# Attention scores in one plain float32 product per head, two heads side by side on the rows of TensorE, and attention under the same list schedule as the layers behind it

## The chip, the core and the metric

The kernel runs on one NeuronCore of a Trainium2 chip. A core has TensorE (PE in the profile, with PEld for its weight loads), VectorE (DVE), ScalarE (ACT), GpSimd (POOL) and SyncE (SP), which issues DMAs here. PSUM has eight banks of 128 partitions by 512 float32. The metric is the device time of one execution in microseconds, lower is better.

## What is computed

Attention with rotary embedding on 2 x 8 heads, 576 positions, 64 features a head; its output, as 1152 tokens by 512 features, goes through two feed-forward layers.

```python
q_rot, k_rot = (rotate(q), rotate(k))
scores = scale * np.matmul(q_rot, k_rot.transpose(0, 1, 3, 2))
scores = scores - np.max(scores, axis=-1, keepdims=True)
attn = np.exp(scores)
attn = attn / (np.sum(attn, axis=-1, keepdims=True) + 1e-09)
return np.matmul(attn, v).astype(np.float32)
...
h = np.maximum(x @ w_in, 0.0)
return (h * h @ w_out).astype(np.float32)
...
a = x @ w_a
b = x @ w_b
return (a * b @ w_out).astype(np.float32)
```

Queries, keys, values and the output are float32; the weights are float64, come as int64 bit patterns and are turned into float32 parts on the chip.

## The kernel before

**Attention** works on eight pairs of heads. The two heads of a pair lie on partitions 0 to 63 and 64 to 127. For each pair the rotated queries and keys are made from `X` (loaded by `load_qk`) by a multiplication with cosines and sines and an addition. From the second pair on this is `prepare` (L305 on): the keys' half on POOL, the queries' half on DVE (L307, L308). Then ACT rounds them to fp32r (`hi`, L309), POOL takes the rest (`lo`, L310), and four DMAs (`place`) put the parts into the tile `sk`, so that the 128 rows of TensorE hold both parts of one head. The first pair does the same by hand in `first_pair` (L316 on), without DMAs.

A pair has nine score blocks (`emit_S`, L365): eight of 128 queries of one head by 576 keys, four matmuls of 288 columns each (two parts of the keys times two banks), and a ninth with the last 64 queries of both heads, ten matmuls. A block goes through a row maximum on DVE (L374) and an exponential on ACT (L380, tile `P`), is transposed on TensorE three blocks later (`emit_T`, `LT = 3`: L435, the odds and ends L445 and L449), copied out of PSUM by ACT or DVE (`evac`), and multiplied with the values (`av_units`: L477 for each head on 64 columns of the array, both heads into the two halves of one bank; L472 for the last 64 keys), first for 384 queries, then for 192. The products of `emit_scale` (L402, L410) spread the reciprocal of the row sums. The transposes and the spreads share two PSUM banks, `av` has two more and the scores four (two blocks).

Only the first three blocks' instructions stand in written order (`in_order`). Behind them the framework's scheduler orders all attention instructions.

**The feed-forward layers** (L660 to L662, L869 to L871) are ordered by `Plan`, a list scheduler in the kernel with costs, due times and buffers (`Plan.order`); what it decides is issued under a manual schedule. It starts where attention ends. Every product is made of three fp32r products. Weights pass through `convert` (three instructions on DVE, two on ACT) and `two_parts`; four of them are made during attention.

Of the kernel before, what the change touches and what calls it, by code (L numbers as in the profile page):

```python
# [16 lines left out]
P = 128  # L17
S = 576
# [9 lines left out]
LT = 3  # L28
DM = 512
NWA = 4  # L30
NWB = 8
NG = 5
NV = 3
LEAD = 40.0
HB = 288

# [11 lines left out]
class Op:  # L48
    def __init__(self, engines, cost, fn, deps, acq, rel, k):
        self.engines, self.cost, self.fn, self.k = engines, cost, fn, k  # L50
        self.deps, self.acq, self.rel = list(deps), list(acq), list(rel)
        self.end = None
# [5 lines left out]
class Plan:  # L58


    HOP = 0.1

    def __init__(self, room):
        self.ops = []
        self.free = {t: [0.0] * n for t, n in room.items()}

    def late(self, *tags, at):
        self.start = at
        for t in tags:
            self.free[t] = [at] * len(self.free[t])  # L70
# [7 lines left out]
    def takes(e, cost):  # L78
        if cost is None:
            return 0.0  # L80
        kind, n = cost[0], cost[1] / 1000
        if kind == "mm":
            return cost[2] * (n / 2.4 + 0.0134)
# [8 lines left out]
    def order(self):  # L92
# [13 lines left out]
        def due(o):  # L106
            stack = [o]
            while stack:
# [10 lines left out]
                late = min((y.due - self.HOP - (2.0 if e == "SP" else 0) for y in nexts[id(x)]), default=clock + 5) - self.takes(e, x.cost)  # L119
                x.due = min(late, x.due) if "PE" in x.engines else late  # L120

# [38 lines left out]
        while True:  # L160
# [5 lines left out]
            for e in engines[1:]:  # L166
                first = None
                for o in open_[e]:
                    if o.end is not None:
                        continue  # L170
                    r = room(o)
                    if r is None:
                        continue
                    s = max(at[e], ready[id(o)], r)
                    if first is None or (s, o.due) < first[:2]:
                        first = (s, o.due, o, e)
# [13 lines left out]
            hop = 0.0 if e == "-" else 2.0 if e == "SP" else self.HOP  # L190
# [25 lines left out]
def attention_moe_moe2_kernel(ctx: ExitStack, tc: tile.TileContext, qk, rope, vm, vt, ident_in, sel_in, w_in, w_out, w_a, w_b, w2_out, out):  # L216
# [3 lines left out]
    xpool = ctx.enter_context(tc.tile_pool(name="xpool", bufs=1))  # L220
    raw = ctx.enter_context(tc.tile_pool(name="raw", bufs=3))
    g2 = ctx.enter_context(tc.tile_pool(name="g2", bufs=2))
    ga = ctx.enter_context(tc.tile_pool(name="ga", bufs=1))
    tmp = ctx.enter_context(tc.tile_pool(name="tmp", bufs=1))
    wa = ctx.enter_context(tc.tile_pool(name="wa", bufs=NWA))

    X = {1: xpool.tile([P, 2, 2, S], F32, tag="x", name="X1")}
    xall = xpool.tile([P, NTB, 2, KC, TB], F32R, tag="x", name="x")
    xb = [xall[:, n] for n in range(NTB)]

    def psum_s(name):
        return ps.tile([P, 2, 512], F32, tag="s", name=name)

    def psum_1(tag, name):
        return ps.tile([P, 512], F32, tag=tag, name=name)
# [761 lines left out]
```

## Time and profile before

| what | us |
| --- | --- |
| median of 3 runs (602.7 to 603.99) | 603.72 |
| the profiled execution | 603.05 |
| its span, first to last instruction | 601.3 |
| PE busy (share of the span) | 574.1 (95%) |
| DVE busy | 450.8 (75%) |
| ACT busy | 341.6 (57%) |
| POOL busy | 257.3 (43%) |

Times of the trace are counted from the first instruction of the span. A row of the timeline gives the start, the time to the modelled end, the engine, the line, the operation and what it writes and reads; an instruction that begins before the one ahead has ended overlaps it, so how long a group holds TensorE is read from its start to the next group's start. A plain float32 matmul leaves two records (two matmuls of one instruction of the kernel), an fp32r matmul one.

### The profile page before, as it was taken

To read this page: it belongs to the slowest core of one execution; us is meant where nothing else is said; L and a number is where in the kernel's file an instruction comes from. 1 tells how busy PE (TensorE), PEld (TensorE's weight loads), DVE (VectorE), ACT (ScalarE), POOL (GpSimd) and SP (SyncE) were. 2 spreads that over 40 slices of the span, in tenths; PEclk is the share of its full clock that TensorE was granted. 3 is DMA by queue.
4 is the path that set the end of the run, shared out by engine and by line. 5 is a ranking of instruction groups with operands and counts; after the bars stand their busy time and mean duration, and the time that the engine had idled before them with its cause. 6 is when DMAs were issued, how large, how long until landed. Compare 5 with 4: busy or idle time off the path is not lost.

```text
span 601.3 us, 9575 instructions
## 1 busy us (share of the span) xinstructions
PE 574.1 (95%) x3554; PEld 505.9 (84%) x3554; DVE 450.8 (75%) x743; ACT 341.6 (57%) x738; POOL 257.3 (43%) x275
## 2 busy tenths in 40 slices
PE   2689999999999999999999999999999999999997
PEld 1557566666758999999999999989999999999986
DVE  5967777767535986884696387999888989897554
ACT  4649667788755876870482155457774555554110
POOL 2755556731122652450252045577554655652100
PEclk9989999999999999999999999999999999999999
DMA  7467575746001354441242031023333232320004
GB/s 244 143 177 198 149 197 127 205 135 179 21 2 67 108 166 153 138 141 35 71 141 71 1 106 36 1 70 99 113 106 105 72 106 71 105 71 2 1 0 158
DMA packets 20682, 61.46 MB, mean 102 GB/s; under 512 B 3337, under 2 KB 3721, under 8 KB 19739
## 3 DMA queue, kind: packets, MB, share of 16 engines
q1 hardware_dynamic: 20491, 59.67, 32.7%
q10 hardware_dynamic: 144, 1.18, 0.6%
q8 instruction: 28, 0.46, 0.3%
q14 instruction: 19, 0.16, 0.1%
HBM read 48.16 MB, written 2.36 MB: 84 GB/s over the span
## 4 chain that ended last, share of the span: by engine, by line
PE 85%; DVE 10%; ACT 2%; issue 1%; DMA 1%; SPq 0%; ACTq 0%; DVEq 0%
PE av L477 7%; PE s L365 7%; PE h L660 6%; PE h L661 6%; PE h L662 6%; PE y L660 5%; PE y L661 5%; PE y L662 5%; PE t L435 4%; PE o L871 4%; PE o L870 4%; PE o L869 4%; PE al L660 4%; PE al L661 4%; PE al L662 4%; DVE X L307 2%
## 5 line engine op out<-in xcount | busy, mean ns | idle before, releaser
L568 POOL TENSOR_TENSOR g<-v,g 128x384 fp32r<-128x384 f32 (+1 forms) x47 | 56.8, 1212 | 60.3 <-ACT g L571 60.2
L365 PE MATMUL s<-sk 128*128 128x288 f32 x336 | 65.7, 325 | 16.4 <-ACT sk L341 10.3
L365 PEld LDWEIGHTS s<-sk 128*128 128x128 f32 x336 | 49.0, 196 | 35.5 <-ACT sk L341 11.2
L374 DVE TENSOR_REDUCE st<-s 128x1 f32<-128x576 f32 x72 | 53.9, 753 | 32.9 <-PE s L365 32.5
L660 PE MATMUL y<-g,w_o 128*128 128x384 f32 (+1 forms) x208 | 66.9, 322 | 0.0
L662 PE MATMUL y<-g,w_o 128*128 128x384 f32 (+1 forms) x208 | 66.9, 322 | 0.0
L661 PE MATMUL y<-g,w_o 128*128 128x384 f32 (+1 forms) x208 | 66.9, 322 | 0.0
L660 PE MATMUL h<-x,w_i 128*128 128x384 f32 x192 | 64.2, 335 | 0.0
L661 PE MATMUL h<-x,w_i 128*128 128x384 f32 x192 | 64.1, 334 | 0.0
L662 PE MATMUL h<-x,w_i 128*128 128x384 f32 x192 | 64.1, 334 | 0.0
L380 ACT ACTIVATE P<-s,st 128x576 f32<-128x576 f32 x72 | 53.7, 746 | 16.7 <-DVE st L374 16.5
L660 PE MATMUL al<-y,w_p 128*128 128x288 f32 x192 | 56.9, 296 | 2.2 <-DVE v L836 2.2
L661 PE MATMUL al<-y,w_p 128*128 128x288 f32 x192 | 56.6, 295 | 0.0
L662 PE MATMUL al<-y,w_p 128*128 128x288 f32 x192 | 56.5, 294 | 0.0
L571 ACT CAST g<-v 128x384 fp32r<-128x384 f32 (+1 forms) x72 | 40.3, 564 | 24.8 <-DVE v L840 17.7
L477 PE MATMUL av<-PT,V 128*64 128x384 f32 (+1 forms) x256 | 50.7, 428 | 0.0
L435 PE MATMUL t<-ident,P 128*128 128x128 f32 x288 | 46.9, 286 | 1.2 <-ACT P L380 1.0
L418 ACT COPY PT<-t 128x512 f32<-128x512 f32 (+1 forms) x57 | 31.7, 556 | 23.3 <-PE t L435 22.6
L709 DVE TENSOR_TENSOR oacc<-o,oacc 128x512 f32<-128x512 f32 (+1 forms) x46 | 31.0, 675 | 17.6 <-PE o L871 17.2
L871 PE MATMUL o<-w,g 128*128 128x512 f32 (+1 forms) x110 | 43.1, 392 | 0.0
L870 PE MATMUL o<-w,g 128*128 128x512 f32 (+1 forms) x110 | 42.9, 390 | 0.0
L869 PE MATMUL o<-w,g 128*128 128x512 f32 (+1 forms) x110 | 42.6, 387 | 0.0
(149 smaller groups left out, 1560.9 us busy)
## 6 DMA issues: line engine op xcount, KB each, us to landing
raw_i<-in_w_in SPq DMA_DIRECT2D x16, 512.0 KB, 3.6
raw_o<-in_w_out SPq DMA_DIRECT2D x16, 512.0 KB, 3.3
X<-in_qk SPq DMA_DIRECT2D x6, 1152.0 KB, 5.2
raw_b<-in_w_b SPq DMA_DIRECT2D x12, 512.0 KB, 3.3
raw_a<-in_w_a SPq DMA_DIRECT2D x12, 512.0 KB, 3.3
raw<-in_w_out SPq DMA_DIRECT2D x12, 512.0 KB, 3.2
sk<-hi_lo SPq DMA_DIRECT2D x14, 432.0 KB, 4.6
sk<-hi_lo SPq DMA_DIRECT2D x14, 288.0 KB, 6.0
```

The lines of the kernel that those rows point to most:

```text
L365: pe.matmul(s[:, b, c:c + n], lhs, rhs, start=(m < 2), stop=(m >= len(mm) - len(cuts)), skip_group_check=(j == 8))
L374: dve.tensor_reduce(out=ST[p][:, 0, j:j + 1], in_=SP[i][:, :, 0:288], op=ALU.max, axis=AX.XY, negate=True)
L380: act.activation(pr[:, h, :].rearrange("p (b n) -> p b n", b=2), SP.pop(i)[:, :, 0:288], AF.Exp, bias=st[:, 0, j:j + 1], scale=1.0, accum_ ...
L435: pe.transpose(t[:, k * P:(k + 1) * P], flat[:, c0:c0 + P], ident)
L477: pe.matmul(AVT[p, r][half(h), 0:n], V[p][:, h, k, :], PT[p][:, h, k, q0:q0 + n], start=False, stop=(k == 3), skip_group_check=True)
L568: e.tensor_tensor(out=out_, in0=a, in1=b, op=ALU.subtract)
L660: pe.matmul(dst, wh, mh, start=first, stop=False, skip_group_check=open_)
L661: pe.matmul(dst, wh, ml, start=False, stop=False, skip_group_check=open_)
L662: pe.matmul(dst, wl, mh, start=False, stop=last, skip_group_check=open_)
L869: pe.matmul(b(), gt[:, 0, c], w[:, 0, d], start=(k == 0), stop=False)
L870: pe.matmul(b(), gt[:, 0, c], w[:, 1, d], start=False, stop=False)
L871: pe.matmul(b(), gt[:, 1, c], w[:, 0, d], start=False, stop=(k == H - 1))
```

## The change

The score product takes the rotated queries and keys as they are, in plain float32: 64 rows of the array for one head, the other 64 for the other head, alternating, into two PSUM tiles (`scores`, L351 of the changed kernel; the last 64 queries of both heads in L346). The rounding, the rest, the DMAs of the parts, `first_pair` and the zero fills are gone. The unit is now a chunk of 128 queries of both heads, four to a pair, and the tail chunk of 64.

From the second pair on POOL does the whole rotation (L317, L318); for the first pair `Plan` divides it between DVE and POOL. All attention instructions become operations of `Plan`, with the costs of the diff, and the list schedule runs from the first instruction to the last. The values are multiplied in two halves of 288 queries, each in two parts (`times_v`, L428, L430), both heads always one behind the other. PSUM holds three score tiles of two banks and two banks for all else (transposes, `av`, spreads). The probabilities have seven buffers; the last pair's spreads come behind the first product of the feed-forward layers. Seven weight slots lie apart from attention's memory instead of four; as before four weights are converted during attention (`EARLY`).

```diff
 H = 2
-LT = 3
 DM = 512
-NWA = 4
-NWB = 8
+NWA = 7
+NWB = 5
+NP = 7
+NS = 3
 NG = 5
 NV = 3
-LEAD = 40.0
 HB = 288
+QS = 192
+EARLY = 4
+GATE = (3, 0)
...
+    HOP = {"PE": 0.25, "SP": 2.0, "-": 0.0}
...
+    STAGS, TTAGS = tuple(f"s{k}" for k in range(NS)), ("t0", "t1")
...
+        if p:
+            for qi in (1, 0):
+                m = pl.op("POOL", ("s", 2 * S), lambda e, qi=qi: e.tensor_tensor(out=x()[:, :, qi, :], in0=x()[:, :, qi, :], in1=cs, op=ALU.mult), [done[qi, 0]])
+                r[qi] = pl.op("POOL", ("s", S), lambda e, qi=qi: e.tensor_tensor(out=rot[:, qi, :], in0=x()[:, 0, qi, :], in1=x()[:, 1, qi, :], op=ALU.add), [m] + war)
+            r[2] = r[0]
...
+    def scores(p, c):
+        rot = ROT[p % 2]
+        if c == 0:
+            rotate(p)
...
+        tail = c == 4
+        s = [Buf(STAGS, {t: (lambda t=t, h=h: ps.tile([P, 2, 512], F32, tag=t, name=f"s{p}_{c}_{h}")) for t in STAGS}) for h in range(1 if tail else 2)]
+        SB[p, c] = s
...
+        def mm(e):
+            k0 = [rot[half(h), 1, :] for h in range(2)]
+            if tail:
+                q0 = (rot[half(0), 0, 512:576], rot[half(1), 0, 0:64])
+                for h, bk, c0, kk, n in ((0, 0, 0, 0, 288), (1, 1, 0, 352, 224), (1, 1, 224, 0, 64), (0, 1, 0, 288, 288), (1, 0, 0, 64, 288)):
+                    pe.matmul(s[0]()[half(h), bk, c0:c0 + n], q0[h], k0[h][:, kk:kk + n], start=True, stop=True, skip_group_check=True)
+            else:
+                for bk in range(2):
+                    for h in range(2):
+                        q0 = rot[half(h), 0, 64 * h + c * P:64 * h + (c + 1) * P]
+                        pe.matmul(s[h]()[:, bk, 0:288], q0, k0[h][:, bk * 288:bk * 288 + 288], start=True, stop=True)
...
+        o = pl.op("PE", ("us", 1.1), mm, [r[1], r[0]] + ([r[2]] if c else []), acq=s)
+        SDONE[p, c] = o
...
+        for h in range(len(s)):
+            j = 2 * c + h
+            m = pl.op("DVE", ("p", S), lambda e, h=h, j=j: e.tensor_reduce(out=st()[:, 0, j:j + 1], in_=s[h]()[:, :, 0:288], op=ALU.max, axis=AX.XY, negate=True), [o])
+            x = pl.op("ACT", ("us", 0.86), lambda e, h=h, j=j: e.activation(
+                PP[:, pr.k, h, :].rearrange("p (b n) -> p b n", b=2), s[h]()[:, :, 0:288], AF.Exp,
+                bias=st()[:, 0, j:j + 1], scale=1.0, accum_out=st()[:, 1, j:j + 1]), [m], acq=[pr] if h == 0 else [], rel=[s[h]])
+            ex.append(x)
...
+    def fill(p, name, blocks, after, outs):
+        b = bank_t(name)
...
-    def prepare(p, engs):
-        x = X[p]
-        for qi in (1, 0):
-            engs[qi].tensor_tensor(out=x[:, :, qi, :], in0=x[:, :, qi, :], in1=cs, op=ALU.mult)
-            engs[qi].tensor_tensor(out=rot[:, qi, :], in0=x[:, 0, qi, :], in1=x[:, 1, qi, :], op=ALU.add)
-            act.copy(hi[qi], rot[:, qi, :])
-            pool.tensor_tensor(out=lo[qi], in0=rot[:, qi, :], in1=hi[qi].bitcast(F32), op=ALU.subtract)
-        place(p)
...
-    def emit_S(i):
-        p, j = divmod(i, 9)
...
-        heads = (j % 2,) if j < 8 else (0, 1)
-        mm = []
...
-        for h in heads:
-            q0 = MAIN[h] + (j // 2) * P if j < 8 else (512, 0)[h]
-            lhs = sk[:, h, q0:q0 + P]
-            cuts = ((0, 0, 288, 0), (1, 0, 288, 288))
-            if j == 8 and h == 1:
-                cuts = ((0, 0, 288, 64), (1, 0, 224, 352), (1, 224, 64, 0))
-            for rhs in (sk[:, h, KOFF[h]:KOFF[h] + S], sk[:, h, LOFF[h]:LOFF[h] + S]):
-                mm += [(b, c, n, lhs, rhs[:, k:k + n]) for b, c, n, k in cuts]
-        for m, (b, c, n, lhs, rhs) in enumerate(mm):
-            pe.matmul(s[:, b, c:c + n], lhs, rhs, start=(m < 2), stop=(m >= len(mm) - len(cuts)), skip_group_check=(j == 8))
...
+    def times_v(p, r, part):
...
+        def mm(e, ks, last):
+            for k in ks:
+                for h in range(2):
+                    pe.matmul(b()[half(h), 0:288], v[:, h, k, :], pt[:, h, k, q], start=(k == 0), stop=False, skip_group_check=True)
+            if last:
+                pe.matmul(b()[:, 0:288], VT[p % 2], ptt[:, q], start=False, stop=True, skip_group_check=True)
...
-        def main(r, k):
-            q0, n = RANGE[r]
-            for h in range(2):
-                pe.matmul(AVT[p, r][half(h), 0:n], V[p][:, h, k, :], PT[p][:, h, k, q0:q0 + n], start=False, stop=(k == 3), skip_group_check=True)
...
+    scores(0, 0)
+    for n, (p, c) in enumerate(order):
+        if n + 1 < len(order):
+            scores(*order[n + 1])
...
+        mid = []
+        if p:
+            mid = [lambda: times_v(p - 1, c // 2, c % 2)] if c < 4 else [lambda: flip(p - 1), lambda: spread(p - 1, 0), lambda: spread(p - 1, 1)]
+        fills = [lambda k=k: turned(p, c, k) for k in range(3 if c == 3 else 2)]
+        if c == 4:
+            mid[:1] and mid.pop(0)()
+        for f in fills:
+            f()
+            if mid:
+                mid.pop(0)()
+        for f in mid:
...
+    for n, (fn, *a) in enumerate(steps):
         fn(*a)
-
...
+        if n == 0:
+            spread(p, 0)
+            spread(p, 1)
+            pl.op(None, None, None, [x for r in range(2) for x in XS[p, r]], rel=[held("g4")])
...
-    in_order = ExitStack()
-    in_order.enter_context(tc.manual_schedule(engines={getattr(mybir.EngineType, e) for e in ("PE", "Activation", "DVE", "Pool")}))
-    pl.run({"PE": pe, "ACT": act, "DVE": dve, "POOL": pool, "SP": nc.sync})
-    in_order.close()
+    with tc.manual_schedule(engines={getattr(mybir.EngineType, e) for e in ("PE", "Activation", "DVE", "Pool")}):
+        pl.run({"PE": pe, "ACT": act, "DVE": dve, "POOL": pool, "SP": nc.sync})
```

On TensorE, in the seventh and eighth pair (`s` scores, `t`, `tk` transposes, `av` the product with the values). Before, around the eighth score block of the last pair and up to its ninth:

```order
L435 MATMUL t_1728<-ident,P_1_1654 128x128 x4
L477 MATMUL av_0_1719<-PT_1467,V_1528 64x384 x4
L365 MATMUL s_1742<-sk_93 128x288 x4
L435 MATMUL t_1750<-ident,P_1_1654 128x128 x4
L445 MATMUL tk_1756<-ident,P_0_1619 128x128
L445 MATMUL tk_1756<-ident,P_1_1654 128x128
L477 MATMUL av_0_1719<-PT_1467,V_1528 64x384 x4
L365 MATMUL s_1764<-sk_93 128x288 x5
```

After, for the last pair, from its third chunk's scores to the next:

```order
L351 MATMUL s_2_0_1350<-rot 128x288
L351 MATMUL s_2_1_1352<-rot 128x288
L351 MATMUL s_2_0_1350<-rot 128x288
L351 MATMUL s_2_1_1352<-rot 128x288
L370 MATMUL t_1_0_1357<-small,P 128x128 x4
L428 MATMUL av_0_1334<-PT_wb,V 64x288 x4
L430 MATMUL av_0_1334<-small 128x288
L370 MATMUL t_1_1_1372<-small,P 128x128 x4
L351 MATMUL s_3_0_1379<-rot 128x288
```

The scores stand in fours of two heads, with a transpose group, half of an `av` and a second transpose group between them. In the third pair of the kernel before, `av` was cut in other places, also between the two heads:

```order
L477 MATMUL av_0_619<-PT_360,V_416 64x384
L402 LDWEIGHTS part_0_605
L402 MATMUL r_0_612<-ident,part_0_605 18x128
L435 MATMUL t_628<-ident,P_1_554 128x128 x4
L477 MATMUL av_0_619<-PT_360,V_416 64x384 x2
```

After, each `av` part is a row of four, as `av_0_1334` above. On DVE at the start of attention, before (`X` and `cs_rot` the rotation, `sk` the parts, `st` the row maxima):

```order
L326 TENSOR_TENSOR X_98<-X_98,cs_rot 128x576 x2
L327 TENSOR_TENSOR cs_rot<-X_98 128x576
L326 TENSOR_TENSOR X_98<-X_98,cs_rot 128x192 x2
L327 TENSOR_TENSOR cs_rot<-X_98 128x192
L342 TENSOR_TENSOR sk_92<-cs_rot,sk_92 64x576
L343 TENSOR_TENSOR sk_92<-cs_rot,sk_92 64x192
L342 TENSOR_TENSOR sk_92<-cs_rot,sk_92 64x576
L343 TENSOR_TENSOR sk_92<-cs_rot,sk_92 64x192
L374 TENSOR_REDUCE st_146<-s_136 128x1
L326 TENSOR_TENSOR X_98<-X_98,cs_rot 128x384 x2
```

After, on DVE from its first instruction, and the shares of POOL behind it:

```order
L323 TENSOR_TENSOR X_77<-X_77,cs_rot 128x576 x2
L323 TENSOR_TENSOR X_77<-X_77,cs_rot 128x192
L324 TENSOR_TENSOR cs_rot<-X_77 128x576
L323 TENSOR_TENSOR X_77<-X_77,cs_rot 128x384
L358 TENSOR_REDUCE st_100<-s_0_0_92 128x1
L358 TENSOR_REDUCE st_100<-s_0_1_94 128x1
```

```order
L323 TENSOR_TENSOR X_77<-X_77,cs_rot 128x192
L324 TENSOR_TENSOR cs_rot<-X_77 128x192
L323 TENSOR_TENSOR X_77<-X_77,cs_rot 128x384
L324 TENSOR_TENSOR cs_rot<-X_77 128x384
L317 TENSOR_TENSOR X_88<-X_88,cs_rot 128x2x576 x2
L318 TENSOR_TENSOR rot<-X_88 128x576 x2
```

The subtractions and roundings into `sk` are gone from the start; half of the first queries' rotation and all of the second pair's (`X_88`) is on POOL. Behind the first product of the feed-forward layers and the last pair's spreads, TensorE's instructions are the same in the same order.

## Rows read from the trace of the kernel before

**Rows 1.** Windows of the span: length, busy time of each engine, PEclk, DMA share, GB/s.

```profile
0.00:10.27 10.27, 0.00 (x0) 0.03 (x1) 4.27 (x8) 3.06 (x5) 3.19 (x14) 1.00 0.72 240
10.27:33.13 22.86, 15.44 (x78) 12.57 (x78) 20.99 (x29) 14.46 (x32) 11.52 (x6) 1.00 0.60 176
33.13:185.85 152.72, 148.54 (x941) 98.18 (x941) 100.17 (x179) 104.04 (x259) 69.07 (x105) 0.99 0.49 132
185.85:601.30 415.45, 410.12 (x2539) 395.14 (x2538) 325.39 (x528) 220.08 (x444) 173.50 (x150) 1.00 0.26 84
```

**Rows 2.** Waits of PE in the feed-forward layers: us in total, times, longest.

```profile
PE al L660 <- DVE v L836: 2.2, 3, 0.9
```

**Rows 3.** Timeline of PE in the seventh and eighth pair.

```profile
151.31 1.43 PE L365 MATMUL s<-sk 128*128 128x288 f32 x10
152.57 0.66 PE L435 MATMUL t<-ident,P 128*128 128x128 f32 x4
...
156.28 0.60 PE L435 MATMUL t<-ident,P 128*128 128x128 f32 x4
156.81 0.55 PE L477 MATMUL av<-PT,V 128*64 128x192 f32 x4
157.28 0.80 PE L365 MATMUL s<-sk 128*128 128x288 f32 x4
157.91 0.60 PE L435 MATMUL t<-ident,P 128*128 128x128 f32 x4
158.35 0.38 PE L445 MATMUL tk<-ident,P 128*128 128x128 f32 x2
...
163.08 0.81 PE L472 MATMUL av<-PTT,vtail 128*128 128x384 f32 x2
163.82 0.22 PE L402 MATMUL r<-ident,part 128*18 128x128 bf16 x1
...
168.44 1.51 PE L477 MATMUL av<-PT,V 128*64 128x384 f32 x8
169.88 1.42 PE L365 MATMUL s<-sk 128*128 128x288 f32 x10
```

**Rows 4.** Timeline of PE in the second and third pair.

```profile
33.13 0.78 PE L365 MATMUL s<-sk 128*128 128x288 f32 x4
...
63.46 0.22 PE L402 MATMUL r<-ident,part 128*18 128x128 bf16 x1 [1.16 <-DVE PT L420]
...
65.97 0.86 PE L477 MATMUL av<-PT,V 128*64 128x384 f32 x2
66.76 0.66 PE L435 MATMUL t<-ident,P 128*128 128x128 f32 x4
```

**Rows 5.** The chain that ended last, around the same wait: start, us, what.

```profile
59.68 3.12 DVE X L307
```

**Rows 6.** Timeline of all engines at the start.

```profile
6.39 0.76 DVE L326 TENSOR_TENSOR X<-X,cs_rot 128x576 f32<-128x576 f32 x1 [1.22 <-DMA X<-in_qk]
...
7.86 0.83 DVE L326 TENSOR_TENSOR X<-X,cs_rot 128x192 f32<-128x192 f32 x2
...
10.27 1.30 PE L365 MATMUL s<-sk 128*128 128x288 f32 x4 [10.27 <-ACT sk L341]
...
15.05 4.28 DVE L343 TENSOR_TENSOR sk<-cs_rot,sk 64x384 fp32r<-64x384 f32 x2
```

**Rows 7.** Groups of instructions, shapes apart: count, busy us, mean ns, idle before.

```profile
L374 DVE TENSOR_REDUCE st<-s 128x1 f32<-128x576 f32 x72 | 53.9, 753 | 32.9 <-PE s L365 32.5
L380 ACT ACTIVATE P<-s,st 128x576 f32<-128x576 f32 x72 | 53.7, 746 | 16.7 <-DVE st L374 16.5
...
L307 POOL TENSOR_TENSOR X<-X,cs_rot 128x1152 f32<-128x1152 f32 x7 | 19.0, 2707 | 10.7 <-DMA X<-in_qk 10.7
L307 DVE TENSOR_TENSOR X<-X,cs_rot 128x1152 f32<-128x1152 f32 x7 | 17.5, 2502 | 0.0
L308 POOL TENSOR_TENSOR cs_rot<-X 128x576 f32<-128x576 f32 x7 | 14.1, 2013 | 0.5
```

More of the change, by code (lines that the diff above doesn't have):

```diff
@@ L81, in takes @@
         kind, n = cost[0], cost[1] / 1000
+        if kind == "us":
+            return cost[1]
         if kind == "mm":
@@ L118, in due @@
                 e = x.engines[0]
-                late = min((y.due - self.HOP - (2.0 if e == "SP" else 0) for y in nexts[id(x)]), default=clock + 5) - self.takes(e, x.cost)
+                late = min((y.due - self.HOP.get(e, 0.1) for y in nexts[id(x)]), default=clock + 5) - self.takes(e, x.cost)
                 x.due = min(late, x.due) if "PE" in x.engines else late
+                if x.soon is not None:
+                    x.due = min(x.due, x.deps[0].due + x.soon)
         for o in ops:
@@ L166, in order @@
             for e in engines[1:]:
+                ok = []
+                for o in open_[e]:
+                    if o.end is None and (r := room(o)) is not None:
+                        ok.append((max(at[e], ready[id(o)], r), o.due, o.k, o, e))
                 first = None
[L168 to L176, printed above, removed]
+                if ok:
+                    near = min(x[0] for x in ok) + self.NEAR
+                    x = min((x for x in ok if x[0] <= near), key=lambda x: (0 if e == "SP" else x[1], x[0], x[2]))
+                    first = (x[0], x[1], x[3], e)
                 if first and (best is None or first[0] < best[0]):
@@ new lines, in attention_moe_moe2_kernel, with held @@
+    MTAGS = tuple(f"m{k}" for k in range(2 * NS))
+    WTAGS = ("wa",) + tuple(f"wb{k}" for k in range(NWB))
+    pl = Plan({
+        "raw": 3, "bits": 2, "sums": 0, "cs": 1, "wa": NWA, "P": NP, "v": NV, "u": 2,
+        **{t: 1 for t in STAGS + TTAGS}, **{t: 0 for t in MTAGS + WTAGS[1:]},
+        "g0": 1, "g1": 1, "g2": 0, "g3": 0, "g4": 0,
+    }, 8.0)
+    FLEX = ("DVE", "POOL")
+    EVAC = ("ACT", "DVE")
+    def held(tag):
+        b = Buf(tag, None)
+        b.at = tag
+        return b
@@ L286, in load_v @@
+    LV, zeros, fixed = {}, [], []
     def load_v(p):
[L287 to L288 removed]
+        war = [AVD[p - 2, 1]] if p > 1 else [zeros[p]]
         t = VT[p % 2]
[L290 to L302 removed]
@@ L557, in attention_moe_moe2_kernel @@
+    XS = {}
+    load_qk_done = {}
     REBIAS = 2.0 ** -112
```

541 lines of the change are left out of this document (237 added, 304 removed).

## The prediction, made before the changed kernel was timed

> **What bounds the kernel now.** I read the windows first, cut at the first score matmul (10.27), at the second pair's first (33.13) and at the first feed-forward matmul (185.85) [rows 1]. Behind 185.85 PE is busy for 410.12 of 415.45 us, and its waits there come to 2.2 us [rows 2]: the feed-forward layers are bound by TensorE, and the change leaves its instructions and their order there as they were. They start when attention's last product is through. So what the change is worth is where that start comes to lie.
>
> In front of it are three stretches: 10.27 us in which PE does nothing, 22.86 us of the first pair with PE busy for 15.44, and 152.72 us with PE busy for 148.54. The last looks full, but busy is not the same as at its pace. The timeline of PE gives the pace: from the ninth score block of the seventh pair to that of the eighth are 169.88 - 151.31 = 18.57 us, with no wait listed between them [rows 3]. Eight such pairs are 148.6 us, and from the first score matmul to the first feed-forward matmul pass 185.85 - 10.27 = 175.6. Some 27 us are waits, a slow start and badly packed products.
>
> Two causes of the latter stand in rows. First, a product with the values for one head without its neighbour holds TensorE for 66.76 - 65.97 = 0.79 us [rows 4], while four of the same width, heads alternating, take 169.88 - 168.44 = 1.44, or 0.72 for two [rows 3]: on 64 columns each, two heads go side by side, and the scheduler's order sometimes parts them. Secondly, DVE's rotation: its queries' half takes 2.5 us a pair [rows 7], once 3.12 in the chain that ended last, and then PE waits 1.16 us for a copy on DVE that stood behind it [rows 5, 4].
>
> **The change, part by part.**
>
> *Scores.* Before, a block of four fp32r matmuls holds PE for 157.91 - 157.28 = 0.63 us and the ninth block for 1.26 [rows 3]: 8 x 0.63 + 1.26 = 6.3 us a pair. After, a pair has ten times two plain float32 matmuls of 288 columns (two in each of four chunks, two in the tail), one head on each half of the rows. No row shows two heads side by side on rows. The nearest rows are the two heads side by side on columns: 0.72 us for two of 384 columns, 157.28 - 156.81 = 0.47 for two of 192 [rows 3]. 288 lies in the middle between them, so I take 0.60; the ends are 0.47 and 0.72. Ten are 6.0 us, 0.35 less than now with what the split blocks cost.
>
> *Changes of the array's form.* A transpose group of four takes 158.35 - 157.91 = 0.44 us when transposes follow, and 156.81 - 156.28 = 0.53 when a product on 64 columns follows [rows 3]: 0.09 us for going to another form. The Trainium skill says the same of the array (TensorEngine Tiling (Array Packing), Key Properties: a change of tiling mode drains TensorE), and by that rule the scores, which now have a form of their own, pay on both sides; the rows show the price for one. After, the transposes are followed by `av` or scores in eight of ten groups, before in about five of nine: three or four more at 0.09 are +0.3 us a pair. If going from scores to transposes costs it too, five more are +0.45, which I leave to the range.
>
> *Transposes, values, spreads.* The same 41 transposes. The values for 2 x 288 instead of 384 and 192 queries have as many columns in all. One flip fewer and one spread more, each 0.22 us at most, as the flip at 163.82 [rows 3]. Nothing. So a pair keeps 18.57 - 0.35 + 0.3 = 18.5 us.
>
> *The start.* DVE's second key multiplication begins at 6.39 when its data is there, and lasts 0.76; a 192-wide multiplication is half of 0.83 [rows 6]; the addition over 576 is again some 0.76. That makes 6.39 + 0.76 + 0.42 + 0.76 = 8.3, while POOL does the other 192 columns. The roundings and subtractions behind that, up to 10.27, are gone. I take 8.7 for the first score.
>
> *The first pair.* TensorE begins slow: the first four score matmuls last 1.30, later ones 0.80 [rows 6, 3], about the ratio of its two levels, 1.2 and 2.4 GHz, though the granted clock reads 1.00 in that window [rows 1]. Two chunks at about double 1.2 bring it to 13.5. From there a chunk costs PE 1.2 + 2 x 0.53 = 2.3 us, DVE two maxima of 0.75 and a copy, ACT two exponentials of 0.75 and a copy [rows 7], all about 2.3: with two slow transposes, four chunks and the gathered transposes PE is at the second pair at about 23. The other path there is POOL: its data, some 2.9 MB at 240 GB/s [rows 1], are in at 12, then two multiplications of 2.71 and two additions of 2.01 [rows 7] end at 21.5. PE is later: 23, against 33.13 [rows 4]. That is 10.1 us won. Of the 22.86 us before, 4.28 were two subtractions on DVE at 15.05 [rows 6] that no longer exist.
>
> *From there to the feed-forward layers.* Seven pairs at 18.5 are 129.5. Of the first pair the values (4 x 0.72 + 4 x 0.47 and their last keys, some 1.1: 5.9), a transpose group and odds remain: 7.4. To this come waits. Before, the same sum with 18.57 is 138 and took 152.7, 14.6 more. DVE no longer rotates (its rotation goes to POOL, 2 x 2.71 + 2 x 2.01 = 9.4 us a pair of 18.5, in which POOL has a pair's time), and the heads stay together. New is that transposes, values and spreads share two banks, and that a queue now keeps the written order. Nothing would be the low end, 14.6 as now the high end; I take 4, half a microsecond a pair. Sum: 23 + 129.5 + 7.4 + 4 = 163.9 for the first feed-forward matmul.
>
> *Behind it.* 415.45 as before; four weights are converted ahead as now, and the last pair's spreads hide behind the first product, whose tokens belong to the first pairs. If a weight came late, the next would be PE's products with `w_out`; twelve products of about 2 us stand in front of them.
>
> Total on the scale of the profiled execution: 163.9 + 415.45 + (603.05 - 601.3 = 1.75) = 581.1; that execution was 0.67 under the median 603.72. I forecast 581, some 22 us or 3.7% less.
>
> **The rivals.**
>
> *No two heads side by side on rows.* Then a score matmul stands alone. A full float32 product of 384 columns takes 163.82 - 163.08 = 0.74, a lone one on 64 columns 0.79 [rows 3, 4]; 288 columns are 0.56 to 0.59, two of them 1.15 instead of 0.60. Ten a pair over seven and a half pairs: +41 us, 622: slower. It decides from 0.60 + 22 / 75 = 0.89 us for two heads on. Against it: the columns do it. The Trainium skill has row tiling at up to twofold for contractions of 64 (same page, Theoretical Speedup); by that rule this rival falls, and no run here shows it yet. Chance 0.06.
>
> *A wait takes the place of the old ones.* With two banks for transposes and values, of which `av` holds one through two chunks, the second transpose group of a chunk waits for the copy of the first, and that may stand behind a maximum of 0.75 just begun. Half of it, 0.37, for each of eight groups is 3 us a pair: 22 over seven and a half, in place of my 4, 599. For it: PE's wait in rows 4 is of this kind. Against it: between the groups lies half an `av`, 1.2 us or more, twice a copy. Chance 0.12, for 593 to 602.
>
> *More than forecast.* Two score matmuls in 0.47 and no waits: -75 x 0.13 - 4, 567. For it: from 192 to 384 columns two heads go from 0.47 to 0.72 only, so a share of each is not the columns', and it may be smaller here. Chance 0.08 below 570.
>
> *Given back behind 185.85,* if the conversions don't keep up with the earlier start: DVE is busy for 325.39 of 415.45 there, so there is room [rows 1]. A few microseconds, in the range; 0.02 for more.
>
> **How the numbers follow.** 0.72 for the forecast, with its own range of 570 to 592. The rivals have 0.06 + 0.12 + 0.08 + 0.02. A range from 570 to 594 leaves out the slow rival, most of the waits and the best case: under 2 in 10. A difference under 0.2% (1.2 us) couldn't be told from none. Faster: 0.72 + 0.08 + 0.12 + part of the rest, 0.92; slower the first rival, 0.06; 0.02 between.
>
> **What would show it.** The second pair's first score at about 23; two score matmuls of both heads holding PE for 0.60; transposes in front of `av` and scores at 0.53; pairs 18.5 apart, evenly; the first feed-forward matmul at about 164 and 415 us behind it. Wrong it would be by scores above 0.89 a couple, by waits of PE for copies of `t` in each chunk, by POOL's rotation arriving after PE is done with the pair before, or by a clock that stays at the lower level through the first pair (then its end comes to 28 instead of 23).

## The result, and the profile after

The change made the kernel slower: 609.72 us (median of 4 runs, 609.17 to 611.03) against 603.86 for the kernel before beside it, ratio 1.0104 with an interval of 1.0083 to 1.0125. The forecast was 581. The profiled execution took 609.85 us, its span 607.7.

The windows of the kernel after, cut like [rows 1] at the first score (9.56), the second pair's first score (27.16) and the first feed-forward matmul (175.84), with one more cut between the two feed-forward layers. Columns as in [rows 1].

```profile
0.00:9.56 9.56, 0.00 (x1) 0.01 (x1) 3.35 (x5) 1.28 (x1) 2.23 (x9) 1.00 0.81 268
9.56:27.16 17.60, 16.89 (x79) 10.61 (x79) 9.49 (x14) 8.90 (x22) 10.12 (x6) 1.00 0.57 198
27.16:175.84 148.68, 137.88 (x932) 81.66 (x931) 91.51 (x153) 95.69 (x226) 67.08 (x68) 0.99 0.21 69
175.84:366.00 190.16, 189.54 (x1122) 189.15 (x1122) 135.89 (x227) 109.18 (x224) 72.35 (x65) 1.00 0.29 98
366.00:607.70 241.70, 227.47 (x1426) 206.97 (x1425) 180.56 (x304) 110.73 (x223) 102.88 (x87) 1.00 0.20 67
```

The same two layers of the kernel before:

```profile
185.85:375.00 189.15, 189.15 (x1118) 189.15 (x1117) 139.40 (x228) 110.05 (x223) 71.08 (x65) 1.00 0.30 98
375.00:601.30 226.30, 220.97 (x1424) 205.99 (x1422) 185.99 (x301) 110.03 (x221) 102.42 (x87) 1.00 0.22 72
```

Attention did become shorter: the first feed-forward matmul comes at 175.84 instead of 185.85, 10.0 us earlier. Then the second feed-forward layer, whose matmuls are the same and in the same order, takes 241.70 instead of 226.30, 15.4 us longer, at a granted clock of 1.00 in both. More than the whole gain is lost there. PE stands for 241.70 - 227.47 = 14.23 us of it, before for 5.33, and is busy for 6.5 more, with the same products. Part of each wait hides there: products of 288 columns start 0.13 us apart, but each is given 0.29 to its modelled end. The listed waits, one line in [rows 2], are now eleven on DVE and ACT; the first three (engine, line, what it waited for: us, times, longest):

```profile
PE m L601 <- DVE v L775: 2.5, 2, 1.5
PE m L601 <- ACT v L754: 0.8, 2, 0.5
PE m L808 <- DVE v L766: 0.8, 2, 0.4
```

DVE, ACT and POOL work no longer there than before (180.56 us of DVE against 185.99), so they are not overloaded. They are late.

In attention, the timeline of PE in the eighth pair answers to [rows 3]:

```profile
150.78 0.30 PE L370 MATMUL tt<-small,P 128*64 128x128 f32 x1 [0.45 <-ACT PT_wb L272]
151.29 0.31 PE L483 MATMUL r<-rows,small 27*128 27x96 bf16 x4 [0.22 <-DVE xf L488]
151.54 1.24 PE L351 MATMUL s<-rot 64*128 64x288 f32 x8
152.71 0.66 PE L370 MATMUL t<-small,P 128*128 128x128 f32 x4
153.29 1.19 PE L428 MATMUL av<-PT_wb,V 128*64 128x288 f32 x8
154.41 0.66 PE L370 MATMUL t<-small,P 128*128 128x128 f32 x4
155.00 1.24 PE L351 MATMUL s<-rot 64*128 64x288 f32 x8
```

The scores of a chunk hold PE for 152.71 - 151.54 = 1.17 us: 0.585 for two heads on one bank. A transpose group holds it for 0.58 to 0.59 wherever `av` or scores follow. The tail blocks (L346) stand at 143.40 and 162.46, so a pair takes 19.06. The two waits in these rows, 0.67 us, are the pair's only ones.

### The profile page after: what moved, and what is told of

Read it like the earlier page. It is cut to its first block, busy times and chain, and to the rows that moved or that the text cites. A ratio compares the mean times of both kernels' runs of the same rounds, so it can differ in the third digit from the quotient of the medians.

```text
span 607.7 us, 9362 instructions
## 1 busy us (share of the span) xinstructions
PE 571.8 (94%) x3554; PEld 488.4 (80%) x3554; DVE 420.8 (69%) x699; ACT 325.8 (54%) x693; POOL 254.7 (42%) x234
## 5 line engine op out<-in xcount | busy, mean ns | idle before, releaser
L601 PE MATMUL m<-y,w_p 128*128 128x288 f32 x224 | 67.3, 301 | 3.5 <-DVE v L775 1.5
L602 PE MATMUL m<-y,w_p 128*128 128x288 f32 x224 | 66.1, 295 | 0.0
L603 PE MATMUL m<-y,w_p 128*128 128x288 f32 x224 | 65.9, 294 | 0.0
L359 ACT ACTIVATE P<-s,st 128x576 f32<-128x576 f32 x72 | 53.0, 743 | 12.4 <-DVE st L358 11.9
L370 PEld LDWEIGHTS t<-small,P 128*128 128x128 f32 x288 | 32.4, 144 | 26.9 <-issue 7.2
L370 PE MATMUL t<-small,P 128*128 128x128 f32 x288 | 47.1, 289 | 3.9 <-ACT PT_wb L272 2.0
L601 PEld LDWEIGHTS m<-y,w_p 128*128 128x128 f32 x224 | 42.0, 188 | 8.5 <-DVE v L775 3.0
L601 PE MATMUL m<-x,w_i 128*128 128x384 f32 x132 | 44.3, 336 | 0.0
L603 PE MATMUL m<-x,w_i 128*128 128x384 f32 x132 | 44.1, 334 | 0.0
L602 PE MATMUL m<-x,w_i 128*128 128x384 f32 x132 | 44.1, 334 | 0.0
L649 DVE TENSOR_TENSOR oacc<-m,oacc 128x512 f32<-128x512 f32 (+1 forms) x46 | 30.6, 675 | 18.7 <-PE m L810 12.7
L602 PEld LDWEIGHTS m<-y,w_p 128*128 128x128 f32 x224 | 42.1, 188 | 1.5
L601 PE MATMUL m<-g,w_o 128*128 128x384 f32 (+1 forms) x132 | 42.3, 320 | 0.6 <-DVE yacc L649 0.6
L603 PE MATMUL m<-g,w_o 128*128 128x384 f32 (+1 forms) x132 | 42.2, 320 | 0.0
L602 PE MATMUL m<-g,w_o 128*128 128x384 f32 (+1 forms) x132 | 42.2, 320 | 0.0
L603 PEld LDWEIGHTS m<-y,w_p 128*128 128x128 f32 x224 | 42.1, 188 | 0.0
L649 DVE TENSOR_TENSOR yacc<-m,yacc 128x384 f32<-128x384 f32 (+1 forms) x40 | 19.5, 511 | 28.5 <-PE m L603 28.5
L317 POOL TENSOR_TENSOR X<-X,cs_rot 128x1152 f32<-128x1152 f32 x14 | 36.9, 2651 | 1.0 <-DMA small<-in_sel 1.0
L601 PE MATMUL m<-y,w_b 128*128 128x288 f32 x112 | 33.7, 301 | 3.2 <-DVE v L775 1.0
```

Of the source, the lines that this page charges most:

```text
L317: m = pl.op("POOL", ("s", 2 * S), lambda e, qi=qi: e.tensor_tensor(out=x()[:, :, qi, :], in0=x()[:, :, qi, :], in1=cs, op=ALU.mult), [done ...
L359: x = pl.op("ACT", ("us", 0.86), lambda e, h=h, j=j: e.activation(PP[:, pr.k, h, :].rearrange("p (b n) -> p b n", b=2), s[h]()[:, :, 0:288 ...
L370: pe.transpose(b()[0:src.shape[1], k * P:k * P + P] if w is None else b()[0:w, k * P:k * P + P], src, ident)
L601: pe.matmul(dst, wh, mh, start=first, stop=False, skip_group_check=open_)
L602: pe.matmul(dst, wh, ml, start=False, stop=False, skip_group_check=open_)
L603: pe.matmul(dst, wl, mh, start=False, stop=last, skip_group_check=open_)
```

## The experiments

**Theory A, against B and C.** In the changed kernel the six feed-forward banks are halves of three two-bank tiles (`MB`). Theory A: an access to one half waits for accesses to the other half of the same tile (a copy by ACT for a product that writes the other bank, or for DVE's addition out of it), and these needless waits make DVE and ACT late, and PE in turn. Theory B: the planner's new rules put DVE's and ACT's work in a worse order. Theory C: the weight slots, now parts of one tile, do it.

*Six tiles of one bank* (`six_banks`). The score tiles get a PSUM pool of their own, which is closed when the first feed-forward bank is wanted; each engine's instructions keep their order, in the two traces too. The new pool for the banks also has an option, `reuse_waits="tile"`, that the changed kernel's lacks; the run after this one tells the two apart.

```diff
-    MB = [lazy(lambda k=k: ps.tile([P, 2, 512], F32, tag=f"s{k}", name=f"m{k}")) for k in range(NS)]
+    MP = lazy(lambda: (att.close(), ctx.enter_context(tc.tile_pool(name="mps", bufs=1, space=bass.MemoryType.PSUM, reuse_waits="tile")))[1])
...
-        return Buf(MTAGS, {t: (lambda k=k: MB[k // 2]()[:, k % 2, 0:width]) for k, t in enumerate(MTAGS)})
+        return Buf(MTAGS, {t: (lambda t=t: MP().tile([P, 512], F32, tag=t, name=name)[:, 0:width]) for t in MTAGS})
```

Expected: 

> The changed kernel with one thing different: the six PSUM banks of the feed-forward layers are six tiles of one bank each, not three tiles of two; the order of every engine's instructions stays the same row for row. Theory A (an access to one bank waits for accesses to the other bank of its tile): the stretch behind the first feed-forward matmul falls from 431.9 us back to 415 to 418, the second layer's stretch from 241.7 to about 227, attention stays at 175.8, the whole comes to about 594. Theory B (the planner's new rules order DVE and ACT worse in the second layer) and theory C (five weight slots share one tile): no change, 609 to 610, second layer still at 241.

Measured: 593.99 us, ratio to the kernel before 0.9851 (0.9833 to 0.9869). The windows of its two layers:

```profile
175.63:365.80 190.17, 189.55 (x1122) 189.17 (x1122) 139.25 (x229) 110.34 (x225) 73.56 (x66) 1.00 0.30 98
365.80:592.60 226.80, 221.52 (x1426) 206.34 (x1425) 179.84 (x301) 109.90 (x222) 105.14 (x87) 1.00 0.21 72
```

Attention ends at the same time (175.63), and the second layer is back at 226.80. Planner, order and weight slots are those of the changed kernel, so B and C fall. What the banks did is seen in the groups of ACT's copies out of PSUM in the second layer (count | busy us, mean ns | idle us before them, and what ended it). First the changed kernel:

```profile
L758 ACT COPY v<-m 128x288 f32<-128x288 f32 x24 | 9.6, 400 | 23.7 <-PE m L603 16.7 <-DVE oacc L649 4.8 <-DVE v L775 1.4
L754 ACT COPY v<-m 128x288 f32<-128x288 f32 x24 | 9.6, 399 | 35.2 <-PE m L603 23.7 <-DVE v L775 7.7 <-DVE cl_a L531 2.2
```

and with six tiles:

```profile
L758 ACT COPY v<-be 128x288 f32<-128x288 f32 x24 | 9.6, 401 | 13.1 <-PE be L603 13.1
L754 ACT COPY v<-al 128x288 f32<-128x288 f32 x24 | 9.6, 400 | 35.3 <-PE al L603 32.4 <-POOL w_b L509 1.8 <-POOL g L509 1.0
```

The copy of `be` needs its product and nothing else. With paired banks it also waits for `oacc` on DVE, an addition that reads the neighbouring bank, and stands 23.7 us in all instead of 13.1.

*The pairs alone, in the kernel before* (`before_pairs`).

```diff
-        return Buf("m", lambda: mps.tile([P, 512], F32, tag="m", name=name)[:, 0:width])
+        return Buf(MTAGS, {t: (lambda k=k: (MB.get(k // 2) or MB.setdefault(k // 2, mps.tile([P, 2, 512], F32, tag=f"m{k // 2}", name=f"m{k // 2}", bufs=1)))[:, k % 2, 0:width]) for k, t in enumerate(MTAGS)})
```

Expected: 

> The kernel before, with its six feed-forward banks as three tiles of two banks, every engine's order unchanged. Theory A: the second layer's stretch grows from 226.3 to about 240, the whole from 603.9 to 616 to 619. Theories B and C: nothing changes, 603 to 605, since planner and weight slots are those of before.

Measured: 618.21 us, ratio 1.0257 (1.0226 to 1.0289). Its second layer, in the windows:

```profile
374.10:615.70 241.60, 227.66 (x1424) 206.59 (x1422) 184.53 (x303) 109.78 (x223) 103.72 (x87) 1.00 0.20 67
```

241.60, as in the changed kernel. Pool options and weight slots are those of before, and in the traces every engine's order is the same but for two neighbouring row maxima at 23.5: the paired tiles alone cost some 15 us. Theory A stands, taken away in one kernel and put into the other.

**Do two heads run side by side on the rows?** Two runs. *Heads apart* (`heads_apart`):

```diff
-                for bk in range(2):
-                    for h in range(2):
+                for h in range(2):
+                    for bk in range(2):
```

Expected: 

> The changed kernel with the four score matmuls of a chunk in the order head 0, head 0, head 1, head 1 instead of alternating. If two heads run side by side on half of the rows each, and only neighbours in the queue do, the chunk's four matmuls take the place of three: 1.17 us becomes about 1.75 (each alone 0.58); over 32 chunks that is 18.6 us, 627 in all, less what waits hide. If the 0.585 us for two heads came from something else than neighbours on different rows (a matmul on 64 rows alone being that short), the chunk stays at 1.17 and the time at 609.7.

*All on one half of the rows* (`one_half`):

```diff
-                        q0 = rot[half(h), 0, 64 * h + c * P:64 * h + (c + 1) * P]
-                        pe.matmul(s[h]()[:, bk, 0:288], q0, k0[h][:, bk * 288:bk * 288 + 288], start=True, stop=True)
+                        q0 = rot[half(0), 0, c * P:(c + 1) * P]
+                        pe.matmul(s[h]()[:, bk, 0:288], q0, k0[0][:, bk * 288:bk * 288 + 288], start=True, stop=True)
```

Expected: 

> The changed kernel with all four score matmuls of a chunk on the first head's 64 rows (the second head's scores are the first's again, so its output isn't the reference's). If two heads share TensorE's time because they sit on different halves of the rows, wherever they stand in the queue, four matmuls on the same half take four times 0.585, 2.34 us a chunk instead of 1.17, and attention grows by some 32 x 1.17 = 37 us. If a plain float32 matmul on 64 rows lasts 0.29 us by itself, the chunk stays at 1.17 and the time at 609.7: then the two heads are not side by side, and it is the half contraction that is cheap.

Measured: 611.26 us for the first (ratio 1.0135, 1.0115 to 1.0155), 651.07 in one run for the second. PE's timeline of a chunk, heads apart:

```profile
118.42 1.25 PE L351 MATMUL s<-rot 64*128 64x288 f32 x8
119.60 0.66 PE L370 MATMUL t<-small,P 128*128 128x128 f32 x4
```

and all on one half:

```profile
156.81 2.21 PE L351 MATMUL s<-cs_rot 64*128 64x288 f32 x8
158.95 0.23 PE L472 MATMUL r<-small,part 128*27 128x128 bf16 x1
```

On one half a chunk takes 2.14 us, on two 1.17: the halves of the rows do work side by side, and the rival of 622 us is refuted. But the order within a chunk didn't matter (1.18): my expectation of 1.75 for heads apart failed. How TensorE reaches the other half past a matmul that waits for its own no run shows. The Trainium skill gives up to twofold for contractions of 64 (TensorEngine Tiling (Array Packing), Theoretical Speedup); the trace agrees, with 2.14 against 1.17.

**The fifth pair.** It takes 24.02 us in the changed kernel, between tail blocks at 79.71 and 103.73, and the sixth 20.61. Its timeline, PE, DVE and POOL apart:

```profile
99.31 0.66 PE L370 MATMUL t<-small,P 128*128 128x128 f32 x4 [1.29 <-DVE xf L272]
...
103.14 0.66 PE L370 MATMUL t<-small,P 128*128 128x128 f32 x4 [2.05 <-ACT PT_wb L272]
103.73 1.53 PE L346 MATMUL s<-cs_rot 64*64 64x288 f32 x10
...
96.16 2.74 DVE L531 TENSOR_SCALAR cl_i<-cl_i 128x512 int32<-128x512 int32 x1
...
99.18 2.74 DVE L532 SCALAR_TENSOR_TENSOR bits_i<-raw_i,cl_i 128x512 int32<-128x512 int32 x1
...
95.80 5.57 POOL L317 TENSOR_TENSOR X<-X,cs_rot 128x1152 f32<-128x1152 f32 x2
```

Two passes that convert a weight on DVE, 0.42 and 0.68 us elsewhere, last 2.74 each beside two of POOL's multiplications. The copies behind them are late, PE waits, and behind the second wait the granted clock falls: 0.64 on the mean from 103.70 to 108.50 (1.00 is 2.4 GHz, the lower level, 0.50, is 1.2). Four runs on this.

*Weights one by one* (`gates`): the first four weights wait for the fourth chunk of pairs 3 to 6.

```diff
-GATE = (3, 0)
+GATE = ((2, 3), (3, 3), (4, 3), (5, 3))
...
-        return wide
+        return EXP[GATE[min(max(count[0], 1), EARLY) - 1]][1]
```

Expected: 

> The changed kernel with the four weights that are converted during attention let in one by one, behind the fourth chunk of pairs 3 to 6 (counted from 1), where POOL's rotation for the next pair is mostly through, instead of all behind the first chunk of the fourth pair. If the 5 us that the fifth pair loses come from DVE's conversion passes that lie beside POOL's rotation (the shift 2.74 us instead of 0.42), that pair falls from 24.0 to about 19.5 and the first feed-forward matmul from 175.84 to about 171.5; the whole to about 605. If they come from the pair's own copies and transposes, the loss stays where it is.

Measured: 609.41 us, ratio 1.0096 (1.0064 to 1.0128), no gain. The loss moved: pairs 4, 5 and 6 take 21.07, 21.07 and 21.05. In the fourth and the fifth a conversion pass (L532) still falls beside a run of two multiplications on POOL and lasts 3.03, and PE waits 1.6 us for a copy behind it; in the sixth the granted clock is 0.61 from 112 to 116 us, behind two waits of half a microsecond.

*POOL's rotation in pieces* (`pieces`, on six banks): each multiplication and addition in pieces of 288 columns.

```diff
-                m = pl.op("POOL", ("s", 2 * S), lambda e, qi=qi: e.tensor_tensor(out=x()[:, :, qi, :], in0=x()[:, :, qi, :], in1=cs, op=ALU.mult), [done[qi, 0]])
...
+                for c in (slice(0, HB), slice(HB, S)):
+                    m = [pl.op("POOL", ("s", HB), lambda e, qi=qi, n=n, c=c: e.tensor_tensor(out=x()[:, n, qi, c], in0=x()[:, n, qi, c], in1=cs[:, n, c], op=ALU.mult), [done[qi, 0]]) for n in range(2)]
```

Expected: 

> The changed kernel with six separate banks, and POOL's rotation of pairs 2 to 8 in pieces of 288 columns (twelve instructions of about 0.75 us a pair instead of four of 1.4 to 2.7). If DVE's conversion passes lose their time because they can't start beside a POOL instruction and wait for its end, none lasts longer than about 1.2 us (now 2.73), the fifth pair falls from 24.0 to 20 to 21, the first feed-forward matmul from 175.6 to about 172, the whole from 594.0 to about 590.5. If the two engines merely slow each other, the passes stay as long, or the loss spreads over more of them, and the time stays at 594.

Measured: 602.8 us, ratio 0.9999 (0.9979 to 1.0019), 8.8 more than `six_banks`. The fifth pair did fall, to 19.74. But the third took 30.37. The timelines of POOL and DVE there:

```profile
51.21 9.79 POOL L317 TENSOR_TENSOR X<-X,cs_rot 128x288 f32<-128x288 f32 x13
...
52.01 9.32 DVE L509 TENSOR_TENSOR x<-xf,x 128x288 fp32r<-128x288 f32 x1 [0.86 <-ACT x L512]
```

A subtraction of 0.46 us lasts 9.32, up to the end of a run of thirteen POOL instructions without a gap. *With that subtraction always on POOL* (`pieces_pool`):

```diff
-        XS[p, r] = two_parts("", 288, lambda: xall[:, 0, k, t], lambda: xall[:, 1, k, t], lambda: xf()[:, q], [m], [])
+        XS[p, r] = two_parts("", 288, lambda: xall[:, 0, k, t], lambda: xall[:, 1, k, t], lambda: xf()[:, q], [m], [], "POOL")
```

Expected: 

> Six separate banks, POOL's rotation in pieces, and the last subtraction of each pair's tokens always on POOL (in the run with pieces alone one of them, 288 columns on DVE, lasted 9.32 us beside a run of thirteen POOL instructions, and the third pair 30.4). If DVE's pass waited there for the whole run of POOL, the third pair falls to about 19.4 and the whole from 602.8 to 590 to 592. If the pieces themselves are the cost (POOL too slow with twelve instructions a pair), the third pair stays long and the time at 600 or above.

Measured: 592.17 us, ratio 0.9805 (0.9787 to 0.9822); the third pair is at 18.98. So DVE's pass, not POOL's pace, was the cost.

*All four weights late* (`late_gate`, on six banks):

```diff
-GATE = (3, 0)
+GATE = (6, 0)
```

Expected: 

> The changed kernel with six separate banks, and the four early weights let in behind the first chunk of the seventh pair instead of the fourth: by then POOL's rotations are nearly through. If DVE's conversion passes cost time only beside a run of POOL instructions, the fifth pair falls from 24.0 to about 19.1, no DVE pass of a conversion lasts over 0.8 us, pairs 7 and 8 stay within 0.5 of 19.06, and the whole comes to 594.0 - 4.9 = about 589. If a pair has no room for the conversions anyway, the loss moves into pairs 7 and 8 and the time stays at 593 to 595.

Measured: 591.33 us, ratio 0.9788 (0.9763 to 0.9812). The fifth pair takes 19.02, and the groups of the two passes are at their own length (first the changed kernel, 60 to 125 us, then this one, 125 to 180):

```profile
L532 DVE SCALAR_TENSOR_TENSOR bits_i<-raw_i,cl_i 128x512 int32<-128x512 int32 x4 | 6.0, 1506 | 0.0
L531 DVE TENSOR_SCALAR cl_i<-cl_i 128x512 int32<-128x512 int32 x4 | 4.0, 996 | 0.0
```

```profile
L532 DVE SCALAR_TENSOR_TENSOR bits_i<-raw_i,cl_i 128x512 int32<-128x512 int32 x5 | 3.4, 683 | 0.1
...
L531 DVE TENSOR_SCALAR cl_i<-cl_i 128x512 int32<-128x512 int32 x5 | 2.4, 473 | 0.0
```

Of the 4.9 us, 2.7 arrived: the eighth pair now takes 20.99, with a granted clock of 0.64 from 146 to 150 us.

**The first pair.** From the first score to the second pair's first score pass 17.60 us instead of 14.3. In PE's timeline a chunk takes 19.85 - 17.67 = 2.18 us until shortly before 20, then 1.2:

```profile
9.56 3.67 PE L351 MATMUL s<-cs_rot 64*128 64x288 f32 x10 [9.56 <-POOL cs_rot L324]
...
17.67 2.25 PE L351 MATMUL s<-cs_rot 64*128 64x288 f32 x8
19.85 1.09 PE L370 MATMUL t<-small,P 128*128 128x128 f32 x8
...
27.16 1.24 PE L351 MATMUL s<-rot 64*128 64x288 f32 x8
```

Matmuls on zeros ahead of the scores, into a bank of the transposes, should tell whether the lower level or the chain of maxima, exponentials and copies sets this. *Seven of them* (`warm`, on six banks):

```diff
+    zero, dry = sb.tile([P, 288], F32, tag="zero", name="zero"), bank_t("warm")
+    z = pl.op("DVE", ("us", 0.2), lambda e: e.memset(zero, 0.0))
+    z = [pl.op("PE", None, lambda e: pe.matmul(dry()[:, 0:288], zero[:, 0:P], zero, start=True, stop=True), [z], acq=[dry] if k == 0 else []) for k in range(7)]
+    pl.op(None, None, None, z, rel=[dry])
     scores(0, 0)
```

Expected: 

> The changed kernel with six separate banks, and seven float32 matmuls of 288 columns on zeros on TensorE from about 1 us on, while it has nothing to do before the first score. If the scores run at the lower of the two levels up to 19 us because TensorE did nothing before 9.5, chunks at 1.2 and transposes at 0.55 come from the first chunk or the second on, the second pair's first score falls from 28.3 to 22 to 24, the whole from 594.0 to about 590. If the first pair is bound by its chain of maxima, exponentials and copies, it stays at 28 and the whole at 593 to 594.

Measured: 595.7 us, ratio 0.9869 (0.9827 to 0.9911): no gain over `six_banks`. They ended 2.45 us before the first score, and the windows give the clock behind that:

```profile
8.00:10.00 2.00, 0.15 (x2) 0.15 (x2) 2.00 (x4) 0.00 (x0) 1.64 (x3) 0.94 0.96 398
10.00:12.00 2.00, 2.00 (x8) 1.04 (x8) 0.21 (x1) 0.00 (x0) 1.92 (x2) 0.50 0.98 362
```

*This and the pieces together* (`pieces_warm`) followed the pieces. Expected: 

> Both of the last two edits on six separate banks: the two gains add, about 587, if each is real; 594 if neither is.

 Measured: 603.43 us, ratio 0.9999 (0.9972 to 1.0026), with the third pair at 30.36.

*Eleven of them* (`warm_eleven`: `range(11)`). Expected: 

> The changed kernel with six separate banks and eleven matmuls on zeros ahead of the first score instead of seven, so that TensorE is busy up to it (with seven it stood for 2.45 us, and the granted clock of the first scores was 0.50). If that gap is what takes the level back, the granted clock stays at 1.00 from 10 us on, a chunk lasts 1.2 from the start, the second pair's first score comes at 22.5 to 24 instead of 28, and the whole at 589 to 590. If the lower level comes with the scores themselves, 0.50 stays and so does 594.

Measured: 592.96 us, ratio 0.9829 (0.9797 to 0.9862), not to be told from `six_banks`. The first chunk was at full pace; then PE waited 1.10 us for POOL's second part of the queries, and the next chunk took 14.82 - 12.00 = 2.82:

```profile
9.66 1.24 PE L351 MATMUL s<-cs_rot 64*128 64x288 f32 x8 [0.61 <-POOL cs_rot L324]
12.00 2.89 PE L351 MATMUL s<-cs_rot 64*128 64x288 f32 x8 [1.10 <-POOL cs_rot L324]
14.82 1.97 PE L370 MATMUL t<-small,P 128*128 128x128 f32 x8
```

*Eleven of them and the late gate* (`late_warm`). Expected: 

> Both of the last two edits: 584 to 586 if each gain is real and they add; 589 if one is; 594 if neither.

Measured: 588.37 us, ratio 0.9745 (0.9718 to 0.9771). It beats the kernel before by 15 us and the changed kernel by 21.

*Two more behind the first chunk* (`warm_between`), where PE had waited 1.10 us:

```diff
     scores(0, 0)
+    z += [pl.op("PE", None, lambda e: pe.matmul(dry()[:, 0:288], zero[:, 0:P], zero, start=True, stop=True)) for k in range(2)]
+    pl.op(None, None, None, z, rel=[dry])
```

Expected: 

> The kernel with six separate banks, the late gate and eleven matmuls on zeros, and two more such matmuls between the first chunk's scores and the second's, where TensorE waited 1.10 us. If that wait takes the level back, the granted clock stays at 1.00 through the first pair, the second and third chunk last 1.2 instead of 2.9, the second pair's first score comes at 22 to 23.5 instead of 27.05, and the whole at 584 to 585.5. If the first pair's work brings the lower level whatever stands ahead of it, 0.50 comes as before and the time stays at 588.

Measured: 588.85 us, ratio 0.9751 (0.9733 to 0.9769), the same as without. Its first pair did what the first theory says:

```profile
12.08 1.83 PE L351 MATMUL s<-cs_rot 64*128 64x288 f32 x8
...
14.87 0.75 PE L351 MATMUL s<-cs_rot 64*128 64x288 f32 x2
15.91 1.23 PE L351 MATMUL s<-cs_rot 64*128 64x288 f32 x6 [0.29 <-ACT P L359]
...
18.10 0.75 PE L351 MATMUL s<-cs_rot 64*128 64x288 f32 x2
...
24.37 1.24 PE L351 MATMUL s<-rot 64*128 64x288 f32 x8
```

The granted clock stays at 1.00 and the second pair begins at 24.37 instead of 27.05, 14.64 us behind the first score; in the profiled executions of `warm_eleven` and `late_warm` the level fell behind the wait. The profiled execution is still 2.67 us ahead at the seventh pair's tail block (134.12 against 136.79) and loses it in the last pairs, where the windows show the lower level twice:

```profile
142.00:146.00 4.00, 3.65 (x18) 2.21 (x20) 3.32 (x8) 2.25 (x7) 0.80 (x1) 0.61 0.30 78
...
162.00:165.00 3.00, 2.67 (x17) 1.77 (x19) 1.35 (x4) 0.86 (x2) 0.80 (x1) 0.72 0.00 0
```

`late_warm` has the same waits there and kept 1.00 in its profiled execution. Whether a short wait is followed by the lower level differs between executions; why, stays open. That holds for the waits of the first pair too: two of the five executions of `late_warm` (586.32 and 587.11 us) and the fastest one each of `warm` (591.44) and `warm_eleven` (591.64) show a granted clock of 1.00 on the mean of the whole span, 2.8 to 6.4 us below the profiled executions of the same kernels (589.90, 597.87 and 596.69), which had 0.50 there. So the medians of these four kernels mix both cases, and filling the wait is not shown to gain time. Among the executions at 1.00 the late gate is worth 4.5 to 5.3 us (587.11 and 586.32 against 591.64), about the 4.9 that were expected of it.

## Why the prediction was wrong

By its own terms (us; the time outside the span is the last line):

| term | forecast | measured |
| --- | --- | --- |
| first score | 8.7 | 9.56 |
| first pair, to the second's first score | 14.3 | 17.60 |
| from there to the first feed-forward matmul | 140.9 | 148.68 |
| feed-forward layers | 415.45 | 431.86 |
| outside the span | 1.75 | 2.15 |
| sum | 581.1 | 609.85 |

**The step that failed** is "*Behind it.* 415.45 as before": 16.4 of the 28.7 us. It rested on the feed-forward instructions and their order on PE staying as they were. They stayed. What changed was what each of them waits for, since the six banks became halves of three tiles; `six_banks` puts it right with the order untouched (592.6 - 175.63 = 416.97 us), and `before_pairs` brings it about alone. The line stood in the diff (`MB[k // 2]()[:, k % 2, 0:width]`), and I read it as the same six banks. With this step put right the kernel still takes 593.99, some 13 us over the forecast; these lie in the terms below. My rival of this place ("given back") had the wrong cause, late conversions, and 0.02. With DVE busy for 325.39 of 415.45 us [rows 1] it had room; being late costs PE without any engine being full.

**Waits from the second pair on**, 4 us forecast, were mis-sized: the stretch took 7.8 longer, and 6.5 of that are the fifth and sixth pair (24.02 and 20.61 against 19.06). I counted DVE's relief from the rotation, but not that its conversion passes would stand beside the rotation on POOL. The signs stood in the trace of before. I read the 4.28 us of two subtractions at 15.05 [rows 6] as work; they lay beside two passes of POOL and ended at 19.33, 0.42 behind the second. And DVE's multiplication of the rotation, 3.12 us in [rows 5], takes 1.36 where POOL has nothing to do:

```profile
14.62 2.61 POOL L307 TENSOR_TENSOR X<-X,cs_rot 128x1152 f32<-128x1152 f32 x1 [10.68 <-DMA X<-in_qk]
17.31 1.60 POOL L308 TENSOR_TENSOR cs_rot<-X 128x576 f32<-128x576 f32 x1
20.03 1.36 DVE L307 TENSOR_TENSOR X<-X,cs_rot 128x1152 f32<-128x1152 f32 x1
```

**The first pair** took 3.3 longer: I let the slow start last for two chunks, to 13.5, and it lasted to about 20. The sign I had named for this, an end at 28, nearly came (27.16). But the level is not the whole miss. With the clock at 1.00 throughout (`warm_between`) the same stretch takes 14.64, where my own terms without the slow start give some 11 (14.3 less 2.4 for the two chunks and about 1 for two transposes); that 14.64 lies near 14.3 is luck. Too small was the chunk, 2.3 us: there chunks come 18.10 - 14.87 = 3.23 apart, since the second head's scores wait for an exponential (`P`, L359) to free one of the three score tiles. I took the work of the busiest engine for the period and left out the chain from scores over maximum and exponential to the next scores. **The first score** came 0.86 late, since POOL's addition for the queries ended last: 0.97 us for 192 columns beside an addition on DVE, where 384 columns take 0.99 two microseconds later.

**Right**: two heads' scores in 0.60 (0.585 measured), side by side on the rows. A pair, 18.5 and half a microsecond of waits, is 19.06; within it the transposes cost 0.58 to 0.59 instead of 0.53 and the scores a little less than thought. The wait for the two shared banks (599) didn't come: the eighth pair's waits are 0.67 us, in two places, not eight. Attention's gain over before, forecast as 21.95 us, was 10.0.

## What to carry to other kernels

Equal order on the bound engine does not mean equal time: where a change repacks buffers, read what each instruction now waits for, above all where several PSUM banks become parts of one tile. Give banks that are in flight at the same time a tile of their own. And before work moves from DVE to POOL, look for DVE passes over SBUF that will lie beside it: what such a pass loses counts as busy time, and shows only against the same pass with POOL idle.

## What the runs showed of the hardware

- A DVE subtraction of 288 columns, 0.46 us alone, lasted 9.32 beside thirteen POOL instructions in a row. The Trainium skill (SBUF — State Buffer, SBUF: two separate sides) has a DVE pass with two SBUF inputs, or in a two-port mode, share a port pair with GpSimd; the one that starts first has it for its whole instruction. The passes of 2.74 us, beside a run of two POOL instructions of 5.57 in all, fit that; the 9.32 us outlast the instruction and go to the end of the run. Why DVE got in between two instructions in one case and not in the other, no run here shows.
- Four score matmuls on two halves of the rows take 1.17 us with heads alternating and 1.18 in the order 0, 0, 1, 1; on one half 2.14.
- The granted clock reads 1.00 in the first pair of the changed kernel, at half the pace; behind matmuls on zeros it reads 0.50 at the same pace. At the start the pace of known groups says more than that column.
